# 192 rows of w_down as 96-row halves inside Strassen, with a fourth PSUM bank per pair, in an adaLN block of a spectral mixer and a SwiGLU feed-forward

## Chip, cores and metric

One core of one Trainium2 chip. The metric is the device time of one execution in microseconds (us), the median over runs.

## What is computed

```python
def _A_ref(x, w_r, w_i):                      # x: 1 x 2048 x 640
    X = rfft2(x.astype(float32))              # over (2048, 640), 321 columns kept
    X = X * (w_r + 1j * w_i)
    return irfft2(X, s=(S, D)).astype(bfloat16)

def _B_ref(x, w_gate, w_up, w_down):          # F = 1728
    return silu(x @ w_gate) * (x @ w_up) @ w_down

sa, ca, ga, sb, cb, gb = six 640-wide pieces of silu(c) @ w_mod
h = _layernorm(x) * (1 + ca) + sa
x = x + ga * _A_ref(h, A_w_r, A_w_i)
h = _layernorm(x) * (1 + cb) + sb
return x + gb * _B_ref(h, w_gate, w_up, w_down)
```

All inputs and the output are bfloat16. The 2048 tokens are 16 tiles of 128 (t = 0 to 15); 640 = 5 x 128; 1728 = 13 x 128 + 64 hidden columns.

## The kernel before

The order of instructions on every engine is written out by hand; each engine works through its own list in that order, and waits at an instruction until what it reads is there and what it overwrites is free.

**Spectral part (0 to 86 us).** The two FFTs are matrix products with tables. In the prologue (0 to 12 us) tables and x are loaded, the modulation columns are computed (`mod_cols`; `one_p_ca`, L433), and the first tiles' statistics are taken on DVE (`stats`, bn_stats L350, L351; `gram`, L368 to L372) and finished on POOL (a pow, L362). For each tile t the forward part (12 to 36 us) transforms along the 640 axis (L320, L323), subtracts the mean (`zout`, L390, DVE), scales a table by 1/std on POOL (`gscale`, L377, L378) and transforms along the tokens of a tile (`s1`, L398 to L401, four 324-column matmuls; copies L407). Behind the last tile SP transposes the result (L504); a DMA, L511, loads the rest of w_mod. The frequency part (36 to 63 us) runs over groups of frequencies: transposes (`t2_pe`, L523), `stage_a` (L551), the product with the filter on DVE (`prod`, L573), `stage_b` (L580), `stage_c` (L601); `ga_mod` (L634, L638) broadcasts the gate row ga over partitions between them. The filter's sums and mirrored rows are prepared by `wsum`, and by the DMAs of `flip` and `flip_edge`. The last loop (63 to 86 us) inverts tile by tile (`s1em` L645, `s1er` L650, copy L653 on ACT, L803 and L806 on PE), adds x on DVE (L808, result x1), and prepares the second layernorm (`ln2_sq` L726 on ACT, `ln2_var` L730 to L732, `ln2_pow` L736 on POOL, `ln2_xn`, a transposing DMA `ln2_tr`, and `ln2_mod` L762 on POOL or L765 on DVE). `wd_fold` (L791, DVE) multiplies rows of w_down by gb.

**Feed-forward part (86 to 255 us)**, in chunks of (first tile, tiles): (0,2), (2,4), (6,4), (10,4), (14,2). The first chunk is plain: 13 hidden blocks of 128 with a gate and an up product each (`gu_plain`, L1031, product L1037), then `down_plain` (L908, L912). The other chunks run two Strassen schemes. `gate_up_pairs` (L1058) makes hidden blocks 0 to 11 of gate and up in groups, by `step(i, g)`: matmuls into banks X, Y, Z, copies on ACT (L1084, L1090, L1097), sums and products on DVE (L1094, L1098, L1101, L1103, L1108). Its right-hand operands are sums of the normalised tokens, `h_sums` and `h_neg` (L996 to L1000, DVE), made in the chunk before. Hidden block 12 is done by `gu_plain` at the end of the chunk, and the last 64 hidden columns by `gu13`: 5 matmuls (L1010) that hold gate and up in one 128-row result; two Silus (L1015, L1017) on ACT and two copies (L1016, L1018) on DVE bring the halves of tokens side by side, ten small DMAs (L1019, L1020) cross partitions, and L1021 multiplies.

`down_pair` (L933) computes two token tiles at once: 12 hidden blocks are split in two halves of six (HK), the 640 outputs in two of 320. Seven products of 6 matmuls each, with sums S1 to S4 of the hidden activations (`a_sum`, L884 to L890, DVE) and T1 to T4 of w_down (`wd_tables`, L864 to L870). The remaining 192 rows (block 12, and the 64 rows of block 13) are 8 further matmuls, with one more sum S12 (L892) and a table W13 (`wd_rest`, L873 to L876): 50 matmuls per pair. Three PSUM banks X, Y, Z (of eight in a ring) hold a pair. ACT copies partial results out (L948, L955, L958, L964), POOL adds three of them to the rows of x1 (L949, L959, L962), and DVE adds the rest when storing (`out_store`, L898; DMA L899). Between the products `nxt(i)` puts the work for what follows on the engines: in the first pair of a chunk `a_sum` for the second pair, in the second pair `ln2_mod` and `h_sums` for the next chunk.

Of the kernel before, what the change touches and what calls it, by code (L numbers as in the profile page):

```python
# [28 lines left out]
IDLE = (3, 6, 1, 2)  # L29

# [125 lines left out]
def adaln_block_kernel(ctx, tc, A_x, A_w_r, A_w_i, B_x, B_w_gate, B_w_up, B_w_down, c, w_mod, out):  # L156
# [116 lines left out]
    nc.sync.dma_start(x_sb[:, 12:16, :], x_v[:, 12:16, :])  # L273
    flip_edge(A_w_i, Wflip[0])
    flip_edge(A_w_r, Wflip[1])
    flip(A_w_r, Wflip[1])
# [53 lines left out]
    if True:  # L330
# [62 lines left out]
        def s1(t, Z, Gs):  # L393
# [4 lines left out]
            nc.tensor.matmul(ar, lhsT=Gs[:, 0, :], rhs=zr, start=True, stop=False)  # L398
            nc.tensor.matmul(ar, lhsT=Gs[:, j, :], rhs=zi, start=False, stop=True)
            nc.tensor.matmul(ai, lhsT=Gs[:, 3 - j, :], rhs=zr, start=True, stop=False)  # L400
            nc.tensor.matmul(ai, lhsT=Gs[:, 0, :], rhs=zi, start=False, stop=True)  # L401
# [27 lines left out]
        t1(0)  # L429
        mps = psum[:, 7, 0:NC5]  # L430
# [12 lines left out]
        stats(0)  # L443
# [8 lines left out]
        gscale(0)  # L452
        stats(3)
        zout(0)
# [4 lines left out]
        for t in range(2, NT + 2):  # L459
# [27 lines left out]
            if t in (13, 15):  # L487
                for lo, hi in ((48, 64),) if t == 13 else ((0, 48), (64, 81)):
                    wsum(Wn, lo, hi, nc.vector)
# [7 lines left out]
    if True:  # L497
# [20 lines left out]
        def t2_pe(slot):  # L518
            ls = groups[slot] + (groups[4] if slot == 3 else [])
            n = len(ls)  # L520
            tp = banks((0, 1, 6, 7)[slot], 1, [8, 128], BF16)
# [3 lines left out]
            if slot == 0:  # L525
                nc.vector.tensor_tensor(B2[:], tp[:, :n, :], SAx[:], ALU.add)
            else:
                nc.scalar.copy(B2[:], tp[:, :n, :])
                nc.gpsimd.tensor_tensor(B2[:, 0:4, 0:1], B2[:, 0:4, 0:1], SA[:, ls[0]:ls[0] + 4].unsqueeze(2), ALU.add)
# [101 lines left out]
        def mod_bc(j, lo, bank, o=0):  # L631
            gps_ = psum[:, bank, o:o + 320]
            for k in range(NC5):
                nc.tensor.matmul(gps_, lhsT=sc_rep[:, k, :], rhs=wm_r[:, k, j, lo:lo + 320], start=(k == 0), stop=(k == NC5 - 1))  # L634
            return gps_

        def ga_mod(lo, bank):
            nc.scalar.copy(ga_bc[:, :, lo // 4:lo // 4 + 80], mod_bc(0, lo, bank).rearrange("p (m r) -> p r m", r=4))  # L638
# [18 lines left out]
        t2_pe(0)  # L657
        t2_pe(1)
# [4 lines left out]
        wsum(Wv, 48, 64, nc.vector)  # L663
# [3 lines left out]
        for g in range(NG + 1):  # L667
# [3 lines left out]
            if g + 2 < NG:  # L671
                PPs[g + 2] = stage_a(g + 2)[0]
            if g == NG - 3:
# [8 lines left out]
            if g in (1, 2):  # L682
                ga_mod(320 * (g - 1), 5 + g)
# [17 lines left out]
    nc.sync.dma_start(Wd_sb[:, 0:13, :], B_w_down[0:1664, :].rearrange("(fc fp) d -> fp fc d", fp=P))  # L701
    for h in range(2):
        nc.sync.dma_start(Wd_sb[64 * h:64 * h + 64, 13, :], B_w_down[1664:1728, :])
# [86 lines left out]
    def wd_fold(f2):  # L790
        nc.vector.tensor_tensor(Wd_sb[:, f2, :], Wd_sb[:, f2, :], gb_bc[:], ALU.mult)  # L791

    if True:
        VTs = {0: s1er(0), 1: s1er(1)}
        nc.vector.tensor_copy(gb_bc[:, 0:320], mod_bc(3, 0, 7))
        for t in range(NT):
            if t and t + 1 < NT:
                s1em(t + 1)
                VTs[t + 1] = s1er(t + 1)
            VT = VTs.pop(t)  # L800
            ops = banks(6 * (t % 2), 2, [4, 256])[:, :, 0:160]
            for h in range(2):
                nc.tensor.matmul(ops[:, 2 * h:2 * h + 2], lhsT=VT[:, 4, :], rhs=RI[:, 1, 2 * h:2 * h + 2, :],  # L803
                                 start=True, stop=False)
                for rr in range(2):
                    nc.tensor.matmul(ops[:, 2 * h + rr], lhsT=VT[:, 2 * h + rr, :], rhs=RI[:, 0, 2 * h + rr, :],  # L806
                                     start=False, stop=(rr == 1))
            nc.vector.scalar_tensor_tensor(x1[:, t, :].rearrange("p (m r) -> p m r", r=4), ops.rearrange("p r m -> p m r"), 1.0,  # L808
                                           x_sb[:, t, :].rearrange("p (m r) -> p m r", r=4), ALU.mult, ALU.add,
                                           accum_out=st2[:, t, 0:1])  # L810
            if t in (8, 11):
                gu_dma(GS[0][:], B_w_gate, t // 11 * 2, 2, t == 8)
            if 1 <= t <= 2:
                ln2_sq(t - 1)
            if t == 3:
                ln2_var(0, 2)
                ln2_pow(0, 2)
            if 4 <= t <= 5:
                ln2_xn(0, t - 4)
            if t == 5:  # L820
                ln2_tr(0)
                load_gu(1024, 1664)
            if t in (7, 9, 11, 13):
                ln2_sq(2 + (t - 7) // 2)
            if t == 10:
                ln2_mod(0)
            if t == 14:
                ln2_var(2, 4)
                ln2_pow(2, 4)
            if t >= 7 and t % 2:  # L830
                wd_fold((13, 0, 1, 2, 3)[(t - 7) // 2])
        for o, n, r, w in ((GS[2], 2, 0, B_w_gate), (UG.unsqueeze(1), 1, 4, B_w_gate), (GS[2], 2, 0, B_w_up), (UG.unsqueeze(1), 1, 4, B_w_up)):
            gu_dma(o[:], w, r, n, w is B_w_gate)

# [13 lines left out]
    S12 = rY.cut(6144, [128], F16)  # L848
    nh = rY.cut(6400, [4, 128])
    W13 = rH.cut(0, [2, 320])  # L850
# [419 lines left out]
```

## Time and profile before

| | us |
|---|---|
| median of 15 runs | 256.52 (255.87 to 257.7) |
| profiled execution | 256.71 |
| its span | 254.9 |

| stage, us of the span | bounds |
|---|---|
| prologue | 0 to 12 |
| forward tiles | 12 to 36 |
| frequency groups | 36 to 63 |
| inverse, x1 | 63 to 86 |
| chunk (0,2): gate/up, down | 86.2 to 100.3, to 107.7 |
| chunk (2,4): gate/up, pairs | 107.7 to 134.9, to 148.5 |
| chunk (6,4) | 148.5 to 175.8, to 189.4 |
| chunk (10,4) | 189.4 to 216.3, to 230.0 |
| chunk (14,2) | 230.0 to 243.8, to 251.7 |
| last sums and stores | 251.7 to 254.9 |

The granted clock of TensorE is 0.998. The engines are PE (TensorE; PEld is its weight loading), DVE (VectorE), ACT (ScalarE), POOL (GpSimd) and SP, which here only issues DMAs. In a timeline each row has the start, the length, the engine, the line, and what is written and read; in square brackets stands the idle time before it and what ended that.

### The profile page before, as it was taken

What the parts mean: (1) busy time and instruction counts of PE and PEld (TensorE: products, weight loads), DVE (VectorE), ACT (ScalarE), POOL (GpSimd) and SP (SyncE); (2) the same over time, 40 slices, a digit from 0 to 9 for tenths busy, and PEclk for the clock granted to TensorE, in tenths of its full rate; (3) what the DMA queues carried; (4) which work ended last, traced back from release to release, by engine and by line L of the source; (5) the groups of instructions that cost most, each with busy time, mean ns of one, the idle gap of its engine ahead of it and who ended that gap; (6) DMA issues with size and microseconds to landing.
All of it is one profiled execution on the core that took longest, in us unless ns stands there. A gap on an engine that the chain in (4) does not pass through costs nothing.

```text
span 254.9 us, 6501 instructions
## 1 busy us (share of the span) xinstructions
PE 244.5 (96%) x2520; PEld 199.4 (78%) x2520; DVE 208.3 (82%) x521; ACT 163.7 (64%) x305; POOL 73.0 (29%) x117
## 2 busy tenths in 40 slices
PE   8899988989999999999999999999999999999984
PEld 3688857979889887778876678886668886769953
DVE  2898888978889998879997996879995788994793
ACT  3788665978778598578963477773357776235730
POOL 4487745845021805000003600001440000440021
PEclk9999999999999999999999999999999999999999
DMA  7989999999999899610005020002411000212001
GB/s 222 390 271 336 298 394 194 246 259 399 319 344 290 223 257 173 133 36 0 3 0 105 29 75 13 3 3 46 96 41 36 3 0 4 51 51 59 4 0 51
DMA packets 46588, 34.78 MB, mean 136 GB/s; under 512 B 22111, under 2 KB 43486, under 8 KB 46174
## 3 DMA queue, kind: packets, MB, share of 16 engines
q1 hardware_dynamic: 44892, 30.36, 42.8%
q0 software_dynamic: 1376, 3.93, 6.8%
q8 instruction: 19, 0.31, 0.5%
q10 hardware_dynamic: 290, 0.08, 0.1%
q14 instruction: 11, 0.09, 0.1%
HBM read 26.80 MB, written 4.72 MB: 124 GB/s over the span
## 4 chain that ended last, share of the span: by engine, by line
PE 69%; DVE 5%; ACT 4%; DMA 3%; SPq 2%; issue 1%; DVEq 0%; ACTq 0%
PE psum L1058 29%; PE psum L933 17%; PE psum L1031 8%; DMA rM<-in_w_mod_dram 3%; PE psum L645 3%; SPq L504 2%; PE psum L803 2%; PE psum L580 2%; PE psum L806 2%; PE psum L912 1%; PE psum L551 1%; DVE rA L898 1%; PE psum L601 1%; PE psum L1010 1%; PE psum L650 1%
## 5 line engine op out<-in xcount | busy, mean ns | idle before, releaser
L1058 PEld LDWEIGHTS <-rW 128*128 128x128 bf16 (+1 forms) x528 | 47.0, 98 | 6.0 <-issue 0.6
L949 POOL TENSOR_TENSOR rM<-rM,rL 128x320 f32<-128x320 f32 x7 | 6.2, 885 | 86.8 <-ACT rL L948 86.8
L1058 PE MATMUL psum<-rE,rW 128*128 128x256 f16 (+1 forms) x192 | 27.7, 259 | 0.2 <-ACT rH L1090 0.2
L1058 PE MATMUL psum<-rW 128*128 128x256 bf16 (+1 forms) x240 | 27.1, 259 | 0.0
L573 DVE TENSOR_TENSOR rM<-psum,rW 128x384 bf16<-128x384 f32 (+2 forms) x42 | 20.4, 542 | 4.6 <-PE psum L551 3.8
L1058 PE MATMUL psum<-rY,rW 128*128 128x256 bf16 (+1 forms) x96 | 24.0, 259 | 0.0
L933 PEld LDWEIGHTS <-rX 128*128 128x128 bf16 (+1 forms) x181 | 16.1, 97 | 9.2 <-issue 1.6
L1031 PE MATMUL psum<-rW 128*128 128x256 bf16 (+1 forms) x170 | 23.2, 291 | 0.0
L933 PEld LDWEIGHTS <-rE 128*128 128x128 f16 x168 | 16.4, 98 | 6.5 <-DVE rE L884 0.2
L933 PE MATMUL psum<-rE 128*128 128x320 f16 x126 | 20.4, 299 | 0.0
L933 PE MATMUL psum<-rA,rX 128*128 128x320 bf16 (+1 forms) x119 | 19.5, 301 | 0.8 <-DVE rX L1037 0.8
L1031 PEld LDWEIGHTS <-rW 128*128 128x128 bf16 x170 | 16.5, 98 | 3.8
L1058 PEld LDWEIGHTS <-rE 128*128 128x128 f16 x192 | 17.4, 98 | 2.3
L1108 DVE TENSOR_TENSOR rX<-rH,rL 128x512 bf16<-128x512 bf16 x21 | 8.9, 425 | 11.7 <-ACT rL L1106 11.5
L736 POOL TENSOR_TENSOR rstd<-rstd,mhalf 128x4 f32<-128x4 f32 (+2 forms) x4 | 4.5, 1120 | 46.5 <-DVE rstd L732 46.5
L1098 DVE TENSOR_TENSOR rX<-psum,rX 128x512 f32<-128x512 f32 x21 | 14.5, 688 | 3.2 <-ACT rX L1097 2.9
L1097 ACT COPY rX<-psum 128x512 f32<-128x512 f32 x21 | 12.3, 587 | 7.2 <-PE psum L1058 7.1
L1094 DVE TENSOR_TENSOR rH<-psum,rW 128x512 bf16<-128x512 f32 x21 | 14.5, 690 | 2.4 <-PE psum L1058 0.6
L1090 ACT COPY rH<-psum 128x512 f32<-128x512 f32 x21 | 12.2, 581 | 6.4 <-PE psum L1058 5.7
L1084 ACT COPY rW<-psum 128x512 f32<-128x512 f32 x21 | 12.3, 586 | 5.8 <-PE psum L1058 5.8
L390 DVE SCALAR_TENSOR_TENSOR rE<-rE,mv,psum 128x648 bf16<-128x648 f32 (+1 forms) x17 | 14.1, 840 | 2.0 <-PE psum L323 1.6
L583 ACT CAST rY<-psum 128x512 bf16<-128x512 f32 (+2 forms) x21 | 11.8, 574 | 5.2 <-PE psum L580 5.1
(203 smaller groups left out, 667.6 us busy)
## 6 DMA issues: line engine op xcount, KB each, us to landing
out_dram<-rA SPq DMA_DIRECT2D x31, 80.0 KB, 1.6
rM<-in_w_mod_dram SPq DMA_DIRECT2D x3, 800.0 KB, 9.0
rA<-in_B_w_down_dram SPq DMA_DIRECT2D x1, 2080.0 KB, 13.7
rX<-in_A_x_dram SPq DMA_DIRECT2D x3, 640.0 KB, 7.2
rM<-in_w_mod_dram SPq DMA_DIRECT2D x1, 1600.0 KB, 8.2
rY<-in_B_w_gate_dram POOLq DMA_DIRECT2D x2, 768.0 KB, 6.7
rW<-in_B_w_gate_dram SPq DMA_DIRECT2D x2, 640.0 KB, 7.0
rW<-in_B_w_up_dram SPq DMA_DIRECT2D x2, 640.0 KB, 7.6
```

Source lines behind the costliest of these rows:

```text
L390: nc.vector.scalar_tensor_tensor(Zv[:, h], Cv[:, h], mv[:, t, 0:1], zps[:, h], ALU.mult, ALU.subtract)
L573: nc.vector.tensor_tensor(PP[:, :, hl], xv[:, :, hl], in1, ALU.mult)
L583: nc.scalar.copy(Y2[:, 0:n, :], yps[:, 0:n, :])
L933: nc.tensor.matmul(o, lhsT=lhsT, rhs=rhs, start=start, stop=stop, skip_group_check=True)
L1031: nc.tensor.matmul(gu[u], lhsT=Wgu[:, u, c5, ff * 128:(ff + 1) * 128], rhs=h2T[:, :, c5, :], start=(c5 == 0), stop=(c5 == NC5 - 1))
L1058: nc.tensor.matmul(o[:, f], lhsT=w, rhs=b, start=(start and f == 0 and i == 0), stop=(stop and f == F - 1 and i == len(ops) - 1), skip_gro ...
L1084: nc.scalar.copy(c0, X)
L1090: nc.scalar.copy(c2, X)
L1094: nc.vector.tensor_tensor(c11, Z, c0, ALU.add)
L1097: nc.scalar.copy(c3, X)
L1098: nc.vector.tensor_tensor(c22, Y, c3, ALU.add)
L1108: nc.vector.tensor_tensor(ato, v4(c11), v4(g21), ALU.mult)
```

## The change

- **w_down's last 192 rows** are two halves of 96 rows (`RK`): rows 1536 to 1631 in block 12, and rows 1664 to 1727 with rows 1632 to 1663 behind them in block 13. They become a seventh pair of blocks in the Strassen product: seven products of 7 matmuls, 49 per pair, with tables T7 (made by `wd_rest`) and sums S7 (`a_sum7`) of 96 rows. S12 and W13 go. A fourth bank W holds the last product of a pair, and POOL adds a fourth partial result to x1, except in the last pair, where DVE does it and W's first two blocks are done early.
- **gate/up.** `gu13` leaves gate and up where the matmuls put them: one Silu, and one DVE product of PSUM rows 64 to 127 with it. `gu_plain`'s block 12 is multiplied in two parts, 96 rows and 32 rows (`half.rest`). In chunk 0 `gu13` is issued ahead of the last x1 tile.
- **down_plain** has 14 matmuls of 128 or 96 rows per result, with no separate 64-row ones.
- **Prologue, last forward tile, first frequency groups, flip edges**: `stats(0)`, `zout(0)`, `wsum`, `ga_mod` and the flips move; `s1` of the last tile is computed in two column halves; `ln2_sq` goes two tiles earlier.

```diff
+    flip(A_w_r, Wflip[1])
     flip_edge(A_w_i, Wflip[0])
     flip_edge(A_w_r, Wflip[1])
-    flip(A_w_r, Wflip[1])
...
-            nc.tensor.matmul(ar, lhsT=Gs[:, 0, :], rhs=zr, start=True, stop=False)
-            nc.tensor.matmul(ar, lhsT=Gs[:, j, :], rhs=zi, start=False, stop=True)
-            nc.tensor.matmul(ai, lhsT=Gs[:, 3 - j, :], rhs=zr, start=True, stop=False)
-            nc.tensor.matmul(ai, lhsT=Gs[:, 0, :], rhs=zi, start=False, stop=True)
+            for h in (slice(0, 4),) if t < NT - 1 else (slice(0, 2), slice(2, 4)):
+                o = slice(81 * h.start, 81 * h.stop)
+                for a, ja, jb in ((ar, 0, j), (ai, 3 - j, 0)):
+                    nc.tensor.matmul(a[:, o], lhsT=Gs[:, ja, :], rhs=zr[:, h], start=(h.start == 0), stop=False)
+                    nc.tensor.matmul(a[:, o], lhsT=Gs[:, jb, :], rhs=zi[:, h], start=False, stop=(h.stop == 4))
...
         t1(0)
+        stats(0)
         mps = psum[:, 7, 0:NC5]
         mod_cols(mps, wm_ca, range(0, 3))
...
         t1(1)
-        stats(0)
         dfwd(0)
...
         gscale(0)
+        zout(0)
         stats(3)
-        zout(0)
...
+                    wsum(Wn, 64, 81, nc.gpsimd)
...
-            tp = banks((0, 1, 6, 7)[slot], 1, [8, 128], BF16)
+            tp = banks(slot % 2, 1, [8, 128], BF16)
...
+        wsum(Wv, 48, 64, nc.vector)
         t2_pe(1)
         PX = [stage_a(0)]
         t2_pe(2)
         PX.append(stage_a(1))
         t2_pe(3)
-        wsum(Wv, 48, 64, nc.vector)
+        ga_mod(0, 6)
+        ga_mod(320, 7, range(3))
         for g in range(2):
...
+            if g == 0:
+                ga_mod(320, 7, range(3, NC5))
...
-    nc.sync.dma_start(Wd_sb[:, 0:13, :], B_w_down[0:1664, :].rearrange("(fc fp) d -> fp fc d", fp=P))
-    for h in range(2):
-        nc.sync.dma_start(Wd_sb[64 * h:64 * h + 64, 13, :], B_w_down[1664:1728, :])
+    nc.sync.dma_start(Wd_sb[:, 0:12, :], B_w_down[0:1536, :].rearrange("(fc fp) d -> fp fc d", fp=P))
+    nc.sync.dma_start(Wd_sb[0:RK, 12, :], B_w_down[1536:1632, :])
+    nc.sync.dma_start(Wd_sb[0:64, 13, :], B_w_down[1664:1728, :])
+    nc.sync.dma_start(Wd_sb[64:RK, 13, :], B_w_down[1632:1664, :])
...
+    T7 = [rE.cut(37888 + 640 * i, [320], F16, parts=RK) for i in range(4)]
+    S7 = [rH.cut(256 * i, [128], F16, parts=RK) for i in range(4)]
...
-        nc.vector.memset(W13[0:64, 0], 0.0)
-        nc.vector.tensor_copy(W13[64:128, 0], Wd_sb[64:128, 13, 0:320])
-        nc.vector.tensor_copy(W13[0:64, 1], Wd_sb[0:64, 13, 320:640])
-        nc.vector.tensor_scalar_mul(W13[64:128, 1], Wd_sb[64:128, 13, 320:640], -1.0)
-
-    def a_sum(ATc, j, i, ks=slice(0, 6)):
-        a11, a12, a21, a22 = (ATc[:, HK * f + ks.start:HK * f + ks.stop, 256 * j + 128 * h:256 * j + 128 * h + 128]
-                              for h in range(2) for f in range(2))
-        s1, s2, s3, s4 = (x[:, ks] for x in (S1, S2, S3, S4))
+        b11, b12 = (Wd_sb[0:RK, 12, 320 * h:320 * h + 320] for h in range(2))
+        b21, b22 = (Wd_sb[0:RK, 13, 320 * h:320 * h + 320] for h in range(2))
+        tt = nc.vector.tensor_tensor
+        tt(T7[0], b12, b11, ALU.subtract)
+        tt(T7[1], b22, T7[0], ALU.subtract)
+        tt(T7[2], b22, b12, ALU.subtract)
+        tt(T7[3], b21, T7[1], ALU.subtract)
...
+    def a_sum7(ATc, j, i):
+        sums(i, S7, *(ATc[0:RK, 12 + f, 256 * j + 128 * h:256 * j + 128 * h + 128] for h in range(2) for f in range(2)))
...
-            if tl % 2 == 0:
-                pops = [[psum[:, next_banks(1), 0:320] for _ in range(2)] for _ in range(2)]
-                for h in range(2):
-                    for s in range(2):
-                        rows = slice(64 * s, 64 * s + 64)
-                        nc.tensor.matmul(pops[s][h], lhsT=ATc[rows, 13, 64 * tl:64 * tl + 128],
-                                         rhs=Wd_sb[rows, 13, 320 * h:320 * h + 320], start=True, stop=False)
             for h in range(2):
-                for fc in range(NFC - 1):
-                    nc.tensor.matmul(pops[tl % 2][h], lhsT=ATc[:, fc, tl * 128:(tl + 1) * 128],
-                                     rhs=Wd_sb[:, fc, 320 * h:320 * h + 320], start=False, stop=(fc == NFC - 2))
-                out_store(t0 + tl, pops[tl % 2][h], h)
+                pop = psum[:, next_banks(1), 0:320]
+                for fc in range(NFC):
+                    rows = slice(0, P if fc < 12 else RK)
+                    nc.tensor.matmul(pop, lhsT=ATc[rows, fc, tl * 128:(tl + 1) * 128],
+                                     rhs=Wd_sb[rows, fc, 320 * h:320 * h + 320], start=(fc == 0), stop=(fc == NFC - 1))
+                out_store(t0 + tl, pop, h)
...
+        W = psum[:, next_banks(1), 0:320]
+        last = t + 2 == NT
+        prod(X, half(0, ta), wd(0, 0), True, True)
         nc.scalar.copy(cps_[0], X)
         nc.gpsimd.tensor_tensor(xa[:, 0:320], xa[:, 0:320], cps_[0], ALU.add)
-        for k in range(3):
-            mm(Z, A12[:, k], B21[:, k])
-        prod(Y, S1, T1)
+        prod(Z, half(1, ta), wd(1, 0), True, ks=range(0, HK))
+        if last:
+            prod(W, half(1, tb), t7(3), True, ks=range(0, 2))
+        prod(Y, s7(0), t7(0), True, True)
         nxt(0)
-        mm(Y, ATc[:, 12, tb:tb + 128], w12(1), stop=True)
         nc.scalar.copy(cps_[1], Y)
-        prod(X, S2, T2, stop=True)
+        prod(Z, half(1, ta), wd(1, 0), stop=True, ks=(HK,))
+        prod(X, s7(1), t7(1), stop=True)
         nxt(1)
         nc.scalar.copy(cps_[2], X)
         nc.gpsimd.tensor_tensor(xb[:, 320:640], xb[:, 320:640], cps_[1], ALU.add)
-        prod(Y, S4, B22)
+        out_store(t, Z, 0)
+        prod(Y, s7(3), wd(1, 1), stop=True)
         nxt(3)
         nc.gpsimd.tensor_tensor(xa[:, 320:640], xa[:, 320:640], cps_[2], ALU.add)
-        prod(X, S3, T3, stop=True)
-        nc.scalar.copy(cps_[3], X)
+        prod(X, s7(2), t7(2), stop=True)
         nxt(2)
-        mm(Y, S12, w12(1))
         nxt(4)
-        mm(Y, r13, W13[:, 1], stop=True)
         out_store(t, Y, 1)
-        for k in range(3, HK):
-            mm(Z, A12[:, k], B21[:, k])
-        mm(Z, ATc[:, 12, ta:ta + 128], w12(0), stop=True)
-        out_store(t + 1, cps_[3], 1)
-        mm(X, ATc[:, 12, tb:tb + 128], w12(0))
-        mm(X, r13, W13[:, 0])
-        if t + 2 < NT:
-            prod(X, A22, T4, stop=True)
-            out_store(t, Z, 0)
-            out_store(t + 1, X, 0)
+        if not last:
+            nc.scalar.copy(cps_[3], X)
+            nc.gpsimd.tensor_tensor(xb[:, 0:320], xb[:, 0:320], cps_[3], ALU.add)
+            out_store(t + 1, cps_[3], 1)
+            prod(W, half(1, tb), t7(3), True, True)
+            out_store(t + 1, W, 0)
         else:
-            out_store(t, Z, 0)
+            nc.vector.tensor_tensor(xb[:, 0:320], X, xb[:, 0:320], ALU.add)
+            out_store(t + 1, X, 1)
             for lo in (0, 160):
-                prod(X[:, lo:lo + 160], A22, T4[:, :, lo:lo + 160], stop=True)
+                prod(W[:, lo:lo + 160], half(1, tb), [w[:, lo:lo + 160] for w in t7(3)], stop=True, ks=range(2, HK + 1))
             for lo in (0, 160):
-                out_store(t + 1, X[:, lo:lo + 160], 0, lo, 160)
+                out_store(t + 1, W[:, lo:lo + 160], 0, lo, 160)
 
...
-        gv = g13.rearrange("p (j s q) -> p s j q", s=2, q=128)
-        f13 = rX.cut(14336, [n // 2, 128], F32)
-        m13 = rX.cut(14336 + 1024, [n // 2, 128])
-        b13 = rX.cut(14336 + 1536, [n // 2, 128])
-        nc.scalar.activation(m13[0:64], gv[0:64, 1], ACT.Silu)
-        nc.vector.tensor_copy(m13[64:128], gv[64:128, 0])
-        nc.scalar.activation(f13[0:64], gv[0:64, 0], ACT.Silu)
-        nc.vector.tensor_copy(f13[64:128], gv[64:128, 1])
-        nc.sync.dma_start(b13[0:64], m13[64:128])
-        nc.sync.dma_start(b13[64:128], m13[0:64])
-        return lambda: nc.vector.tensor_tensor(ATc[:, 13, 0:64 * n], f13[:].rearrange("p j q -> p (j q)"),
-                                               b13[:].rearrange("p j q -> p (j q)"), ALU.mult)
+        sg13 = rX.cut(14336, [512], F32, parts=64)[:, 0:128 * n]
+        nc.scalar.activation(sg13, g13[0:64], ACT.Silu)
+        return lambda: nc.vector.tensor_tensor(ATc[0:64, 13, :], g13[64:128], sg13, ALU.mult)
...
+                if ff < 12:
+                    nc.vector.tensor_tensor(ATc[:, ff, :], gu[1], sg[:, 0:N], ALU.mult)
+                else:
+                    nc.vector.tensor_tensor(ATc[0:RK, 12, :], gu[1][0:RK], sg[0:RK, 0:N], ALU.mult)
+
+        half.rest = lambda: nc.vector.tensor_tensor(ATc[64:RK, 13, :], gu[1][RK:P], sg[RK:P, 0:N], ALU.mult)
...
         half(0)
         step(6, nG - 1)
+        q1, q2, q3, q4 = (lambda q=q: a_sum7(ATc, 0, q) for q in range(4))
         if n == 2:
-            step(5, nG - 1)
+            step(5, nG - 1, True)
+            half(1)
+            step(8, nG - 1)
             step(7, nG - 1)
             s3, s4 = later
             r1, r2, r3, r4 = (lambda q=q: a_sum(ATc, 0, q, slice(2, 6)) for q in range(4))
-            later[:] = [r1, r2, s4, r4, s3, r3]
-            half(1, lambda: run(2))
+            later[:] = [r1, half.rest, q1, r2, q2, s4, r4, q4, s3, r3, q3]
         else:
             queue(nG - 1)
             half(1, lambda: run(len(later) - 2))
-            run(2)
-            step(5, nG - 1)
-            step(7, nG - 1)
+            later[:0] = [half.rest, q1, q2]
+            later.extend([q3, q4, lambda: step(8, nG - 1), lambda: step(7, nG - 1)])
+            step(5, nG - 1, True)
         run(len(later))
-        a_sum(ATc, 0, 4)
...
+            if t == NT - 1:
+                fin13 = gu13(0, at_of(0))
...
+            if t in (5,7,9,11):
+                ln2_sq(2 + (5,7,9,11).index(t))
...
-                    if n == 4:
+                    if n == 4 and i < 4:
                         a_sum(ATc, 1, i)
+                        a_sum7(ATc, 1, i)
```

## The prediction

> **What bounds the kernel now.** I read the busy shares first, then the chain of waits, then what PE waits for, and last the windows of the feed-forward part and its timelines, because the change sits mostly there.
>
> ```profile
> PE 244.5 (96%) x2520; PEld 199.4 (78%) x2520; DVE 208.3 (82%) x521; ACT 163.7 (64%) x305; POOL 73.0 (29%) x117
> ```
>
> TensorE works for 244.5 of 254.9 us, so only about 10 us are idle and every matmul taken away counts almost in full, if nothing new makes PE wait. The chain of waits (start, length, what) shows where PE doesn't set the pace:
>
> ```profile
> 45.61 8.16 DMA rM<-in_w_mod_dram
> 53.81 0.28 PE psum L555 x5
> ...
> 84.26 0.59 ACT rL L653
> 84.89 0.31 PE psum L803
> ...
> 110.31 0.44 DVE rX L1016
> 110.77 0.38 ACT rX L1017
> 111.15 0.48 ACT rH L1090
> ```
>
> So the frequency stage hangs on a weight load that ends at 53.81; the end of the x1 loop waits for an ACT copy; and the 64-row rest of gate/up costs a little DVE/ACT ping-pong. The windows of the second chunk's two down pairs and of the next two pairs (window, length, busy us of PE, PEld, DVE, ACT and POOL, then clock, DMA share and GB/s):
>
> ```profile
> 134.90:141.70 6.80, 6.80 (x51) 4.68 (x50) 5.08 (x13) 1.70 (x4) 3.91 (x4) 1.00 0.52 99
> 141.70:148.50 6.80, 6.80 (x51) 4.81 (x51) 6.70 (x16) 4.60 (x8) 2.82 (x4) 1.00 0.16 49
> ...
> 175.80:182.60 6.80, 6.80 (x51) 4.67 (x50) 6.49 (x14) 1.71 (x4) 3.15 (x3) 1.00 0.51 96
> 182.60:189.40 6.80, 6.80 (x51) 4.81 (x51) 6.73 (x15) 3.87 (x7) 2.91 (x3) 1.00 0.16 51
> ```
>
> PE is full, but DVE is nearly full too in the second pair of each chunk (6.70 and 6.73 of 6.80). What DVE hasn't done by then (the next chunk's normalised tokens L765 and their sums L996 to L1000) PE needs in the next chunk's second step. And POOL isn't free beside DVE. Timelines of the two engines at the first pair:
>
> ```profile
> 139.10 0.85 POOL L949 TENSOR_TENSOR rM<-rM,rL 128x320 f32<-128x320 f32 x1
> 139.92 0.85 POOL L959 TENSOR_TENSOR rM<-rM,rL 128x320 f32<-128x320 f32 x1
> 140.75 1.17 POOL L962 TENSOR_TENSOR rM<-rM,rL 128x320 f32<-128x320 f32 x1
> ...
> 139.15 0.83 DVE L743 SCALAR_TENSOR_TENSOR nb<-st,rstd 128x6 f32<-128x6 f32 x1 [1.44 <-POOL rstd L736]
> 139.90 1.30 DVE L884 TENSOR_TENSOR rE<-rX 128x768 f16<-128x768 bf16 x1
> 141.30 1.03 DVE L886 TENSOR_TENSOR rE<-rE,rX 128x768 f16<-128x768 f16 x1
> 142.43 0.56 DVE L890 TENSOR_TENSOR rE<-rX,rE 128x768 f16<-128x768 bf16 x1
> ...
> 147.70 0.41 DVE L996 TENSOR_TENSOR rE<-rW 128x512 f16<-128x512 bf16 x1
> ...
> 149.28 0.29 DVE L1000 TENSOR_SCALAR rE<-rE 128x512 f16<-128x512 f16 x1
> ```
>
> The same 768-element sum takes 0.56 alone and 1.03 to 1.30 while a POOL add is under way.
>
> **What the Trainium skill says.** "SBUF — State Buffer", section "Who interferes with whom": a GpSimd instruction that reads SBUF and a DVE instruction with two SBUF inputs take the shared port in turn, the first blocks the other; a DVE source in PSUM isn't in it. The trace agrees: 0.56 becomes 1.03 to 1.30, and the PSUM store L898 keeps its 0.48. "TensorE: Matmul & The Clock Gate", section on LDWEIGHTS: the load is set by columns, not contraction rows, so a 96-row matmul should cost what a 128-row one does; in this trace the 64-row L933 matmuls run at nearly the 320-column pace of 0.136.
>
> **Part by part**, against the profiled execution (256.71, span 254.9; 0.19 over the median of 256.52).
>
> Prologue. The statistics of tile 0 (two bn_stats and an aggregate, 7.48 to 8.60, so 1.1) go ahead of one_p_ca L433, before which DVE idles 0.57: L433 is some 0.5 later. The first z (L390, 0.84) goes ahead of statistics 3, so the pow for tiles 2 and 3 and the second gscale come later on POOL. The first s1 matmuls follow that at 12.04 and 13.72, from where PE runs without a break. Between 0 (it is absorbed before 13.72) and +0.8; I take +0.5.
>
> The last s1 (t=15) in column halves can start when half of z is there; four 324-column matmuls stood behind L390's second half. Half of their 0.56: −0.27. Its ACT copies, SP's transposes and the load ending at 53.81 all follow it, so it is carried through; 0 if that load is bound by something else.
>
> First frequency groups, flip order on SP, and the sums moved to POOL: PE waits for the load at 53.81 whatever stands before it. The ga_mod matmuls (0.7 each) move, none is added. Cost 0; the cover is that load.
>
> Rest of gate/up for chunk 0 (L1010, 5 matmuls, 0.55) goes ahead of the last x1 tile. PE waits there 0.38 for L653, and two ACT squares (L726, 0.6 each) have left that stretch. Its input, POOL's L762, ends at 84.64, just in time: −0.5 (0 to −0.55).
>
> Down_plain: 4 row-tiled 64-row matmuls in 0.38 plus 52 become 56, of 0.136 each: 4 × 0.136 − 0.38 = +0.16.
>
> Rest of gate/up in the Strassen chunks: L1016, L1017, L1018, L1021 and ten small DMAs become one Silu and one DVE product from PSUM; PE's small gaps at 111.6 and 152.5 (matmuls start 0.24 and 0.34 later than the pace gives) close: −0.4 (0 to −0.6).
>
> Pairs: 50 matmuls become 49. A pair took 13.64/2 = 6.82, so 0.136 goes from each of the six full pairs: −0.84 with rounding (−0.8).
>
> Tail: the last pair has 2 full and 10 half-width matmuls for W where 12 half ones stood, S12 (0.88 beside POOL) is gone and so is a wait of PE for L1037 in part (0.78 at 247.06); against it stand four small sums and an added DVE add on X. −0.3, from −0.8 to +0.2.
>
> Without new stalls this is 0.5 − 0.27 − 0.5 + 0.16 − 0.4 − 0.84 − 0.3 = −1.65.
>
> Now DVE. In the stretch of a chunk's pairs L1016/L1018/L1021 are gone (1.3, but early in the chunk where DVE has time). New at the end of gate/up: the gate/up product of block 12 falls apart into a 96-row and a 32-row one, with the fixed cost and PSUM width of L1037 again: +0.6. The last c12 sum and its product (steps 8 and 7) go behind these; with four tiles they serve only the second pair, so 0. New: four 96x128 sums for each pair in place of one (L892, 0.21, net 0.14): +0.42 a pair. New on POOL: a fourth 128x320 add per pair, 0.86, which can hold up one sum (0.47 to 0.56 of delay).
>
> Walk for chunk 1 (pairs begin at P0 = 134.88). The +0.6 and +0.42 come ahead of the variance L730 to L732, so the pow L736 (1.32 on POOL) ends at about 140.1, where it ended at 139.1. The adds L949, L959, L962 and the new one are queued behind it, the sums for pair 1 behind L743 on DVE, which waits for pow. From 140.1 on four adds of 0.86 (3.4) alternate with four sums of 0.47 and four small ones of about 0.15 (2.5) and two stores (0.8): all done at 146.8. The fourth product needs its sum at P0 + 10.5 = 145.4, the fifth at 146.8: PE waits about 1.2 in pair 1 already. Then the stores, L765 (149.3 where it was 145.51, 2.3 long beside POOL) and L996 to L1000 (1.75) end at 153.3. PE needs them at 150.69 − 0.3 = 150.4. So a loss of 2.9 by the end of it (the 1.2 is in it). Bounds: 0.8, if POOL lets two DVE operations through between its adds, and 3.2.
>
> Chunk 2 has no pow in its way: L765 would begin at P0 + 10.65 for 7.96 and the sums end at P0 + 15.95, needed at 15.53: +0.45 (0 to 1). Chunk 3 has 3.0 of slack at this place (L1000 ends 228.6, needed 231.6): 0 (to 0.3).
>
> Sum: −1.65 + 2.9 + 0.45 = +1.7; 256.71 + 1.7 = 258.4, on the median's footing 258.2.
>
> **The rivals.** A, on the other side: DVE keeps up. It is decided at 150.4, where PE reads L999's and L1000's sums: if DVE is through them by then, PE never waits and the saved matmuls stay saved. For it: the small sums may slip in while PSUM-source operations run, and DVE has 1.7 us of idle in the first pair's window (5.08 of 6.80). Against: that idle is the wait for pow, which gets later. Time: 256.52 − 1.65 = 254.9.
>
> B: half of the stall, because two DVE operations run between POOL's adds: −1.65 + 1.7 = about 0, 256.6. For it: in the trace of before the four sums took 139.90 to about 143.4, 3.5 for 1.9 of work, so three adds cost 1.6 or 0.55 each, not 0.86; four would cost 2.2, and the sums end at 145.6. Against: before, only two of the four sums (L884, L886) met adds at all, and the new small ones give every add a partner.
>
> C: everything at its bad end: prologue +0.8, tail +0.2, stalls 3.2 + 1 + 0.3: 0.8 − 0.27 − 0.5 + 0.16 − 0.4 − 0.84 + 0.2 + 4.5 = +2.65, about 259.3; a fourth PSUM bank per pair (the ring of eight holds only two pairs) can make PE wait for a store on top.
>
> **How the numbers follow.** Forecast 0.45, A 0.24, B 0.13, C 0.18. A is faster, B is split (0.03 faster, 0.08 same, 0.02 slower, since 0.2% or 0.5 us is what a measurement here can tell), the forecast and C are slower but for 0.03 of same: faster 0.27, same 0.11, slower 0.62. Predicted 258.2. The range runs from A's time to above C's: 254.8 to 259.8; the forecast's own is 257.2 to 259.2.
>
> **What would show it.** Right: PE waits for DVE (L884 to L890's new sums, or L996 to L1000) at 145 to 153, two to three us in all, and for nothing at 84.9; POOL's adds and DVE's sums alternate at 140 to 146; chunk 1's pair 0 lasts 6.7. The forecast falls if the second chunk's pairs keep to 13.4 us and the third chunk starts without a wait, or if PE's idle time sits in the prologue or in a bank that isn't free yet.

## The result, and the profile after

| | before | after |
|---|---|---|
| median, us | 256.66 (47 runs) | 260.0 (9 runs) |
| ratio | | 1.0123, interval 1.0104 to 1.0142 |
| profiled execution's span | 254.9 | 258.2 |

The change makes the kernel slower by 1.2%, 3.3 us. The forecast was slower by 1.7 us, in a range that ended at 259.8: the direction and the largest term were right, the sum was about half of what came.

Where the two executions part can be read from a few instructions that both have. The table gives their start, and what the difference grew by in each stretch, beside what the prediction's terms add up to for it.

| first instruction of | before | after | grown by | predicted |
|---|---|---|---|---|
| the matmuls that need the last w_mod load (L555, now L561) | 53.81 | 55.10 | +1.29 | +0.23 |
| gate/up of chunk 0 (L1031, now L994) | 86.00 | 86.72 | −0.57 | −0.5 |
| gu13 of chunk 1 (L1010, now L982) | 108.17 | 108.97 | +0.08 | +0.16 |
| pairs of chunk 1 (L933, now L903) | 134.88 | 135.35 | −0.33 | −0.2 |
| pairs of chunk 2 | 175.77 | 178.66 | +2.42 | +2.42 |
| pairs of chunk 3 | 216.32 | 219.22 | +0.01 | +0.17 |
| the last pair | 243.76 | 246.66 | 0.00 | −0.28 |
| end of the span | 254.9 | 258.2 | +0.4 | −0.3 |

Three stretches went otherwise than predicted: the first, the end, and, smaller, the pairs of chunks 2 and 3. At the first row the load is later, and so is PE. The last w_mod load was issued at 46.06 and took 8.7, so it landed at about 54.8 (before: 45.61 and 8.2, so 53.8). PE came to it only at 55.10 and waited for nothing there:

```profile
55.10 0.27 PE L561 MATMUL psum<-sc_col,rM 128*128 128x1 bf16 x5
```

So about 1.0 of the 1.29 lay in the load whatever PE did before it, and 0.3 in PE's own delay behind the ga_mod matmuls, whose wait of 2.0 is the first in the list below. The page's first part after:

```profile
PE 245.8 (95%) x2516; PEld 200.7 (78%) x2516; DVE 214.8 (83%) x538; ACT 162.8 (63%) x299; POOL 81.1 (31%) x124
```

DVE works 6.5 us more than before and POOL 8.1 more. PE is idle for 2.0 us more, and busy for 1.3 us more although the change takes matmuls away; for some 3 us its clock was halved (last section). What PE waits for, after (total, times, longest):

```profile
PE psum L640 <- DMA rM<-in_w_mod_dram: 2.0, 1, 2.0
PE psum L1026 <- DVE rE L972: 1.1, 1, 1.1
...
PE psum L903 <- DVE rE L857: 0.8, 1, 0.8
PE psum L557 <- DVE rM L532: 0.7, 1, 0.7
PE psum L903 <- ACT rL L935: 0.4, 2, 0.2
```

L857 and L972 are the sum for the fifth product of chunk 1's second pair and the negation of the next chunk's token sums: the two waits that the prediction named. L640 (the ga_mod matmuls, which waited for nothing before) and the wait for L935 (an ACT copy) are new. The timelines of POOL, DVE and PE after, at chunk 1's pairs:

```profile
139.85 1.33 POOL L747 TENSOR_TENSOR rstd<-rstd,mhalf 128x6 f32<-128x6 f32 x1 [38.39 <-ACT rL L935]
141.16 0.85 POOL L925 TENSOR_TENSOR rM<-rM,rL 128x320 f32<-128x320 f32 x1
141.98 1.24 POOL L936 TENSOR_TENSOR rM<-rM,rL 128x320 f32<-128x320 f32 x1
143.19 1.31 POOL L940 TENSOR_TENSOR rM<-rM,rL 128x320 f32<-128x320 f32 x1
144.46 1.18 POOL L947 TENSOR_TENSOR rM<-rM,rL 128x320 f32<-128x320 f32 x1
145.59 1.18 POOL L925 TENSOR_TENSOR rM<-rM,rL 128x320 f32<-128x320 f32 x1
...
141.96 0.55 DVE L853 TENSOR_TENSOR rE<-rX 128x768 f16<-128x768 bf16 x1
142.43 0.88 DVE L853 TENSOR_TENSOR rH<-rX 96x128 f16<-96x128 bf16 x1
143.23 0.54 DVE L855 TENSOR_TENSOR rE<-rE,rX 128x768 f16<-128x768 f16 x1
143.70 0.88 DVE L855 TENSOR_TENSOR rH<-rH,rX 96x128 f16<-96x128 f16 x1
...
146.77 1.22 DVE L857 TENSOR_TENSOR rE<-rX 128x768 f16<-128x768 bf16 x1
147.92 0.88 DVE L857 TENSOR_TENSOR rH<-rX 96x128 f16<-96x128 bf16 x1
...
148.05 0.99 PE L903 MATMUL psum<-rE 128*128 128x320 f16 x6 [0.82 <-DVE rE L857]
...
154.00 0.61 PE L1026 MATMUL psum<-rE 128*128 128x256 f16 x4 [1.08 <-DVE rE L972]
```

The pow (L747) ends at about 141.17 and all adds queue behind it back to back, into the second pair's own. Beside them the 96x128 sums take 0.88 each, four times the 0.21 that they take alone. The fifth product (the one with the third sum; products are counted as in the prediction, without Z's) needs the sum L857, which is done at 147.99, and its small part at 148.8, while PE stands.

### The profile page after: what moved, and what is told of

Read it like the earlier page. It is cut to its first block, busy times and chain, and to the rows that moved or that the text cites. A ratio compares the mean times of both kernels' runs of the same rounds, so it can differ in the third digit from the quotient of the medians.

```text
span 258.2 us, 6499 instructions
## 1 busy us (share of the span) xinstructions
PE 245.8 (95%) x2516; PEld 200.7 (78%) x2516; DVE 214.8 (83%) x538; ACT 162.8 (63%) x299; POOL 81.1 (31%) x124
## 5 line engine op out<-in xcount | busy, mean ns | idle before, releaser
L1026 PEld LDWEIGHTS <-rW 128*128 128x128 bf16 (+1 forms) x528 | 47.0, 98 | 6.0 <-issue 0.7
L1026 PE MATMUL psum<-rE,rW 128*128 128x256 f16 (+1 forms) x192 | 27.7, 259 | 0.0
L1026 PE MATMUL psum<-rW 128*128 128x256 bf16 (+1 forms) x240 | 27.2, 259 | 0.3 <-DVE rW L776 0.2
L1026 PE MATMUL psum<-rY,rW 128*128 128x256 bf16 (+1 forms) x96 | 23.9, 259 | 0.0
L903 PEld LDWEIGHTS <-rE 128*128 128x128 f16 x168 | 16.1, 97 | 9.2 <-DVE rE L857 1.1
L994 PE MATMUL psum<-rW 128*128 128x256 bf16 (+1 forms) x170 | 23.2, 291 | 0.0
L903 PE MATMUL psum<-rE 128*128 128x320 f16 x126 | 20.7, 299 | 1.6 <-DVE rE L857 0.8
L1026 PEld LDWEIGHTS <-rE 128*128 128x128 f16 x192 | 17.3, 98 | 3.6 <-DVE rE L972 1.4
L994 PEld LDWEIGHTS <-rW 128*128 128x128 bf16 x170 | 16.5, 98 | 3.8
L747 POOL TENSOR_TENSOR rstd<-rstd,mhalf 128x4 f32<-128x4 f32 (+2 forms) x4 | 4.5, 1121 | 47.0 <-ACT rL L935 38.4
L903 PEld LDWEIGHTS <-rX 128*128 128x128 bf16 (+1 forms) x152 | 14.4, 97 | 5.6 <-DVE rX L1003 0.5
L903 PE MATMUL psum<-rA,rX 128*128 128x320 bf16 (+1 forms) x98 | 15.7, 299 | 0.0
L1026 PE MATMUL psum<-rE,rY 128*128 128x256 f16 (+1 forms) x96 | 15.1, 259 | 0.0
```

Of the source, the lines that this page charges most:

```text
L903: nc.tensor.matmul(o, lhsT=lhsT, rhs=rhs, start=start, stop=stop, skip_group_check=True)
L994: nc.tensor.matmul(gu[u], lhsT=Wgu[:, u, c5, ff * 128:(ff + 1) * 128], rhs=h2T[:, :, c5, :], start=(c5 == 0), stop=(c5 == NC5 - 1))
L1026: nc.tensor.matmul(o[:, f], lhsT=w, rhs=b, start=(start and f == 0 and i == 0), stop=(stop and f == F - 1 and i == len(ops) - 1), skip_gro ...
```

## The experiments

Each kernel ran beside the kernel before on the same chip; ratios are against it.

**1. ga_mod back in its place.** In the changed kernel the ten matmuls of ga_mod were returned to behind the second and third stage_b.

```diff
-        ga_mod(0, 6)
-        ga_mod(320, 7, range(3))
...
+            if g in (1, 2):
+                ga_mod(320 * (g - 1), 5 + g)
```

> The changed kernel with the ga_mod matmuls put back to where they were (5 each behind the second and third stage_b). Theory: in PE's list they stand ahead of stage_a(2), so everything behind them waits for the w_mod piece that lands at 41.5; and after 2 us of idle PE runs at half clock for 4 us. Then the frequency stage gives back 1.2 to 1.6 us (first stage_c matmul at about 45.1 where it is 47.64 now) and the kernel about 1.3. Rival: stage_a(2) would be late anyway, since DVE's filter sum took 2.05 beside POOL's and the next one waited for a mirrored row block until 39.10; then at most 0.4 us comes back.

Measured: 260.38, ratio 1.015 (1.0109 to 1.019); the changed kernel had 1.0123. The 1.3 us that the theory gave did not come: PE no longer waits at 41.5, the first stage_c matmul starts at 44.73 (expected 45.1), but then PE stands 1.87 us at the last w_mod load:

```profile
54.34 0.28 PE L561 MATMUL psum<-sc_col,rM 128*128 128x1 bf16 x5 [1.87 <-DMA rM<-in_w_mod_dram]
```

So that load covers all but some tenths of the move, much as predicted. What was overlooked is that the load itself is later.

**2. pow early.** The variance, pow and nb of tiles 10 to 15 go into the third and fourth group of chunk 1's gate/up, where POOL has nothing to do.

```diff
+            if ci == 1 and p == 2:
+                ln2_var(10, 6)
+                ln2_pow(10, 6)
+            if ci == 1 and p == 3:
+                ln2_nb(10, 6)
...
-        if ci == 1:
-            ln2_var(10, 6)
-            ln2_pow(10, 6)
-            ln2_nb(10, 6)
```

> The changed kernel with the variance, pow and nb of tiles 10 to 15 computed in the middle of chunk 1's gate/up, not ahead of its pairs. Theory: pow ahead of POOL's adds is what pushes all adds and sums of the pairs late, 141.2 where they could start from 137; without it the waits in pair 1 (0.98) and in the next chunk's step 2 (1.9) go for the larger part: 2 to 2.8 us less. Rival: it is the number of adds and sums in itself (DVE and POOL alternate, 8 sums and 4 adds per pair); then the waits shrink by under 1 us.

Measured: 256.92, ratio 1.0013 (0.9996 to 1.003): by the ratios 2.8 us less than the changed kernel, nearly the whole loss. In the profiles, chunk 1 from the start of its pairs to that of chunk 2's lasts 40.58, where it lasted 43.31 in the changed kernel and 40.89 before. PE waits for neither L857 nor L972 any more. POOL's adds now stand apart, each started when ACT's copy is there:

```profile
141.66 0.86 POOL L947 TENSOR_TENSOR rM<-rM,rL 128x320 f32<-128x320 f32 x1 [0.70 <-ACT rL L946]
143.62 0.86 POOL L925 TENSOR_TENSOR rM<-rM,rL 128x320 f32<-128x320 f32 x1 [1.11 <-ACT rL L924]
145.39 0.88 POOL L936 TENSOR_TENSOR rM<-rM,rL 128x320 f32<-128x320 f32 x1 [0.91 <-ACT rL L931]
```

The number of adds and sums is the same, so it is their time that cost 2.8 us. The edit moves two things at once: POOL's adds no longer stand behind the pow, and DVE's sums no longer behind nb (L754), which waited 1.45 for that pow. How much each of the two counts was not separated.

**3. Both of these at once.**

> Both edits at once. They lie in different stages, so the gains add up: theory 3.3 to 4.2 us, 255.8 to 256.7; rivals of both: under 1.4 us, 258.6 or more.

Measured: 257.74, ratio 1.0068 (1.0048 to 1.0087). A miss: 0.8 us slower than pow early alone, so beside the early pow ga_mod's new place is rather a gain. About half of this kernel's executions had a mean granted clock of 0.992 or 0.993, and of those all but one took 258.1 to 259.6, where most of the others took 257.1 to 257.7. The profiled one, at 256.66 the fastest of all, shows a clock of 0.50 from 40.6 to 44.0 and the first stage_c at 46.44 (44.73 in experiment 1), but the last load, passed at 54.16, hides most of that. Why the old place costs here stays open.

**4. The kernel before with ga_mod moved as in the change.**

> The kernel before with nothing but the ga_mod matmuls (and the banks of the transposes that they need) moved as in the change. Theory: the same loss as in the changed kernel, 1.2 to 1.6 us by the first stage_c and PE at half clock around 42 to 45. Of that a part is hidden, since PE waits 1.2 us at 53.81 for the next load anyway: so 0.2 to 0.6 us in the time. Rival: no loss, because the load is there in time when the mirrored rows go in the old order.

Measured: 257.04, ratio 1.0012 (0.9989 to 1.0034): no loss that can be told, though the interval doesn't exclude the theory's 0.2 to 0.6. The trace sides with the rival: PE waits 0.9 at the first piece and then 0.7 at the last load, where it waited 1.2 at that alone, its clock stays at 1.00, and the first stage_c starts at 44.95 for 44.97.

**5. Flips in the old order**, in the changed kernel.

```diff
-    flip(A_w_r, Wflip[1])
     flip_edge(A_w_i, Wflip[0])
     flip_edge(A_w_r, Wflip[1])
+    flip(A_w_r, Wflip[1])
```

> The changed kernel with the flip edges back ahead of the second flip on SP. Theory: that order is what makes every later transfer of SP's queue late by half a us to one us: the first w_mod piece is then issued at 30.7 where it is 31.2 now and lands at 40.7 (41.5), PE's wait for it shrinks from 2.0 to about 1.1 so that the clock isn't cut, and the last w_mod load lands at 53.7 (54.3): 0.6 us less, or up to 1.3 where the clock was cut. Rival: SP's order is without effect, since the loads are limited by the DMA engines' total work; then under 0.2 us.

Measured: 258.66, ratio 1.0073 (1.0038 to 1.0108), 1.3 us less than the changed kernel; the two intervals just touch. From SP's queue the first flip edge, the w_mod transfers and the transposes, changed kernel first, then this one:

```profile
13.19 5.01 SPq L262 DMA_DIRECT2D wflip_i<-in_A_w_i_dram  x1
...
20.26 0.58 SPq L278 DMA_DIRECT2D rM<-in_w_mod_dram  x1
...
31.20 0.57 SPq L286 DMA_DIRECT2D rM<-in_w_mod_dram  x1
37.12 8.89 SPq L509 DMA_TRANSPOSE rL<-rA  x3
46.06 1.00 SPq L516 DMA_DIRECT2D rM<-in_w_mod_dram  x1
```

```profile
12.60 0.95 SPq L262 DMA_DIRECT2D wflip_i<-in_A_w_i_dram  x1
...
17.21 1.80 SPq L278 DMA_DIRECT2D rM<-in_w_mod_dram  x1
...
30.72 0.62 SPq L286 DMA_DIRECT2D rM<-in_w_mod_dram  x1
37.22 7.98 SPq L509 DMA_TRANSPOSE rL<-rA  x3
45.24 0.85 SPq L516 DMA_DIRECT2D rM<-in_w_mod_dram  x1
```

The same three transfers stand ahead of L278 in both orders, but behind the second flip the issue of the first edge takes 5.0 us and not 0.95, and L278 goes out 3 us later. Most of this is made up again; the piece for ga (L286) is still issued 0.5 earlier in the old order, the transposes behind it finish 0.8 earlier, though they are issued later, so the last load (L516) goes out 0.8 earlier and PE gets to it at 53.38.

All 14 profiled kernels agree on the beginning: with the new order (7 kernels) the first edge took 4.5 to 5.0 and L278 was issued at 19.7 to 20.3; with the old order (7 kernels, before among them) 0.95 and 16.3 to 17.2. Further on the two groups come close: the piece for ga was issued at 30.7 to 31.2 and PE passed the last load at 53.6 to 55.1, mean 54.3, for 29.8 to 30.7 and 53.0 to 53.8, mean 53.3.

What an earlier load is worth depends on the next wait. In this profiled execution, the slowest of five (259.77), PE is 1.7 us ahead at the last load, but at gu13 of chunk 0 it waits for POOL's `ln2_mod`, 1.0 in three times, and at the first gate/up matmul only 0.24 is left:

```profile
84.75 0.27 PE L982 MATMUL psum<-rW,Wp 128*128 128x256 bf16 x1 [0.45 <-POOL rW L773]
```

**6. The new flip order alone, in the kernel before.**

> The kernel before with nothing changed but the second flip ahead of the flip edges. Theory: this order alone delays what follows in SP's queue: the piece for ga is issued 0.5 us later (31.2 for 30.7), the last w_mod load lands at 54.3 to 54.5 for 53.8, so 0.5 to 1 us slower. Rival: in the kernel before the order is hidden and only the other edits make it count; then within 0.2 us.

Measured: 257.07, ratio 1.0028 (1.0017 to 1.0039): 0.7 us slower by the ratio, the size that the theory gave. Its profiled execution doesn't show the theory's path: the first edge takes 4.54, but the piece for ga is issued at 30.68 (30.66 before) and the load passed at 53.88 (53.81). So the time bears out that the order costs something; on which path, this trace leaves open.

**7. A place of its own for the third copy.** In the changed kernel, cps_[2] goes to bytes 9216 on, which nothing uses any more there.

```diff
-    cps_ = [rL.cut((2560, 10496, 0, 1280)[i], [320], F32) for i in range(4)]
+    cps_ = [rL.cut((2560, 10496, 9216, 1280)[i], [320], F32) for i in range(4)]
```

> The changed kernel with the third copy of a pair (ACT, cps_[2]) in a place of its own. Theory: it shares bytes with the Silu results g21/g22 that step 7 reads; step 7 now stands behind the small sums on DVE, so ACT's copy waits for it, and PE waits for the copy ahead of the pair's fifth product, 0.36 us in each of chunks 2 and 3 (in chunk 1 a longer wait hides it): 0.7 us less, PE waits for the copy gone. Rival: the copy would wait for something else as late (POOL's adds, DVE's sum for that product), then 0 to 0.2 us.

Measured: 259.03, ratio 1.0096 (1.0065 to 1.0126), by the ratios 0.7 us less than the changed kernel, as the theory has it; the intervals overlap, so the trace has to decide. In the changed kernel, at chunk 2's first pair, DVE, ACT and PE read:

```profile
182.78 0.47 DVE L1075 TENSOR_TENSOR rX<-rH,rL 128x512 bf16<-128x512 bf16 x1
...
183.34 0.43 ACT L935 COPY rL<-psum 128x320 f32<-128x320 f32 x1 [1.31 <-DVE rX L1075]
...
183.81 0.97 PE L903 MATMUL psum<-rE 128*128 128x320 f16 x6 [0.20 <-ACT rL L935]
```

L1075 is step 7, which reads g22, and g22 begins in the bytes that the copy overwrites. PE's fifth product starts 0.50 after the last matmul of the fourth, where the pace is 0.14: 0.36 lost. With the copy elsewhere the wait is gone, and this pair lasts 6.70 (178.09 to 184.79) instead of 7.06 (178.66 to 185.72). Chunk 3 is shorter by the same 0.36.

**8. The fourth add on DVE.** In the changed kernel, for the full pairs.

```diff
-            nc.gpsimd.tensor_tensor(xb[:, 0:320], xb[:, 0:320], cps_[3], ALU.add)
+            nc.vector.tensor_tensor(xb[:, 0:320], X, xb[:, 0:320], ALU.add)
```

> The changed kernel with the fourth partial sum of the full pairs added by DVE from PSUM (0.4) and not by POOL. Theory: POOL's adds and DVE's sums take turns, so one add less in the first pair of chunk 1 brings the later sums forward by 0.8 to 1.2 and costs DVE 0.4: PE's waits in chunk 1 shrink by 0.3 to 0.8 us. Rival: what counts is DVE's own work; then 0.4 more for each pair whose sums are late, 0.4 to 0.8 us slower.

Measured: 259.18, ratio 1.0113 (1.0081 to 1.0145). PE's wait for L972 shrank from 1.1 to 0.5, that for a sum stayed at 0.8; from chunk 1's pairs to chunk 2's it is 42.67 for 43.31. The trace bears the theory out; the total is no different from the changed kernel's within the interval. One add less relieves a little, where the pow's place gives nearly all.

**9. pow early in the kernel before.**

> The kernel before with the pow of tiles 10 to 15 in the middle of chunk 1's gate/up. Theory: before had 1.1 us of slack at that place, PE never waited there, so nothing changes (within 0.2 us), though DVE's wait of 1.44 for pow goes; the place of pow costs only beside the new sums and adds. Rival: pow's place costs by itself (POOL's adds late, stores late): 0.5 us less or more.

Measured: 255.96, ratio 0.9992 (0.9968 to 1.0015): no change that can be told, though the interval alone doesn't exclude the rival's 0.5. The trace does: from chunk 1's pairs to chunk 2's it is 40.63 for 40.89. The pow was in the same place before and cost no more than these 0.26, because its delay ended inside the slack.

**10. Three repairs at once**: pow early, flips in the old order, own place for the copy.

> Three repairs at once: pow early, flips back, own place for the third copy. Theory: they lie in different places and add up, and with pow early the copy's wait counts in all three chunks (3 x 0.36): 256.9 - 0.6 - 1.0 = 255.3, faster than before by 0.4%. Rivals: if only the pow matters, 256.9; if the flips alone help, 256.3.

Measured: 254.98, ratio 0.9932 (0.9906 to 0.9958). Faster than before by 0.7%, 5 us better than the change as it was. In the list of PE's waits one alone is left from chunk 1 on, 0.4 in the last pair. Here the saved matmuls show: from pairs to pairs chunks 1, 2 and 3 last 40.19, 40.20 and 27.08, for 40.89, 40.55 and 27.44 before.

**11. The last pair in another order**, on top of 10: the fifth product and its DVE add ahead of the fourth. With it, the third sums come ahead of the fourth ones on DVE, and Z and W each have four blocks done early; this part of the edit is left out here.

```diff
+            prod(X, s7(2), t7(2), stop=True)
+            nc.vector.tensor_tensor(xb[:, 0:320], X, xb[:, 0:320], ALU.add)
+            out_store(t + 1, X, 1)
+            prod(Y, s7(3), wd(1, 1), stop=True)
+            out_store(t, Y, 1)
```

> The same with the last pair in another order: the fifth product ahead of the fourth, so that DVE's add of it falls into DVE's idle 1.05 us and not ahead of the last stores. Theory: the tail is bound by DVE (add 0.4, stores 0.4 and 2 x 0.27 behind the last products), so 0.4 to 0.6 us less than the kernel beside it, 254.8. Rival: the end is set by the first sums of that pair (PE waits 0.7 for them) and by the last transfer, then 0 to 0.2.

Measured: 255.05, ratio 0.9938 (0.9922 to 0.9953): no gain over 10, as the rival had it. From the pair's first matmul to the end of DVE's last store 8.45 us passed for 8.65: the add and all four stores still stand one behind another at the end (247.82 to 249.78).

**12. Without the last add**, on top of 10.

```diff
-            nc.vector.tensor_tensor(xb[:, 0:320], X, xb[:, 0:320], ALU.add)
```

> The kernel with the three repairs, with the last pair's DVE add of the third product's sum into x1 left out (that part of the last tile's output lacks it). Theory: DVE is the bound behind the last products, so its 0.40 comes off whole. Rival: the last matmuls or the transfers on SP set the end, 0 to 0.15 us.

Measured: 254.6, ratio 0.9927 (0.9905 to 0.9948); the interval can't tell 0.4 us from nothing, but the trace can. With the add, then without it:

```profile
247.86 0.49 DVE L873 TENSOR_TENSOR rA<-psum,rM 128x320 bf16<-128x320 f32 x1 [1.05 <-POOL rM L940]
248.27 0.48 DVE L952 TENSOR_TENSOR rM<-psum,rM 128x320 f32<-128x320 f32 x1
248.67 0.94 DVE L873 TENSOR_TENSOR rA<-psum,rM 128x320 bf16<-128x320 f32 x3
```

```profile
249.08 1.35 DVE L873 TENSOR_TENSOR rA<-psum,rM 128x320 bf16<-128x320 f32 x4 [1.05 <-POOL rM L940]
```

DVE waits for POOL's last add (L940), and from there its work follows without a gap, so DVE is the bound. It ends 8.65 us after the pair's start with the add (240.96 to 249.61) and 8.25 without (242.18 to 250.43): 0.40, and the span from the pair's start to the end is 0.3 shorter.

## Why the prediction was wrong

**Right: the stall in chunk 1, with its place and its total.** Predicted was +2.9 by a chain through pow, POOL's adds and DVE's sums. The stretch grew by 2.42 where the terms gave 2.42, and PE's matmuls start later than the pace of the first pair (6.70) gives: by 1.6 up to the end of the pairs, and by 1.2 more at L1026. The steps between are off: the sums of pair 1 end at 148.8 and not 146.8, since the pow ended later and three of the second pair's adds joined in, and `ln2_mod` (L776) took 1.69 for 2.3 and made a part of it up. So the exact total is partly luck. Experiment 2 takes nearly the whole of the stall away by moving variance, pow and nb, and experiment 9 shows that their place costs next to nothing without the new sums and adds. The 96-row matmuls keep the pace of 0.14, as the prediction took it.

Rival B (half of the stall) is out by size, but its picture holds in part: at the first two adds a small and a large sum do run for each, a round of 1.27 where the two take about 0.6 alone. An estimate from this is 0.67 for an add, between the forecast's 0.86 and B's 0.55. Rival A, no stall, came only with experiments 2 and 10.

**Wrong: "Cost 0; the cover is that load."** This was said of the first groups, the flips and ga_mod together. The step looked at PE's list and not at the queue that the cover itself stands in: the load landed 1.0 later. At the matmuls that need it the difference was +1.29 where +0.23 was predicted. For ga_mod the cover held, but for the last 0.3 in this execution (experiments 1 and 4). For the flips it did not: experiments 5 and 6 put 1.3 and 0.7 us on their order. What is shown of the way there is the flip edge of 4.5 to 5.0 us in SP's queue; how it comes to 1 us at the last load is not. Part of the 1.29 belongs to the two profiled executions: before's was the latest of its group, after's the latest of its own.

**Wrong: steps 8 and 7 behind the sums, "so 0".** I asked who reads their result, and not whose bytes they read. A copy that needs those bytes became late and PE with it, 0.36 in the first pairs of chunks 2 and 3 (experiment 7). It ate up the saved matmuls there. **Wrong the other way: chunk 2, +0.45.** That stall didn't come: in experiment 7, without the late copy, the stretch to the pairs of chunk 3 lasts 40.19 for 40.55 before. The two errors nearly cancel: +0.01 and 0.00 grew where +0.17 and −0.28 were expected.

**Mis-sized: the tail, −0.3, measured +0.4.** Behind the last products DVE has one add more (0.40, experiment 12), and the last stores wait for DVE, not for PE. That is 0.4 of the 0.7; the rest is open. The prediction's bad end was +0.2.

**Mis-sized, the other way: the prologue, +0.5.** In the traces the first s1 starts at 11.86 for 12.04 before, and the second at 13.54 for 13.72: no loss here. (Of the ten profiled kernels with the change eight start it by 12.12, two at 12.58 and 13.61; this was not followed up.) The split of the last s1 gave less than its 0.27: its transposes start 0.31 earlier, but 0.18 of this was there at the first s1. The term for gu13 of chunk 0 (−0.57 for −0.5) holds as long as POOL's `ln2_mod` is in time, which it is not in experiment 5.

**The range.** Its upper end was set by rival C, whose sum is wrong by 1: the terms 0.8 − 0.27 − 0.5 + 0.16 − 0.4 − 0.84 + 0.2 + 4.5 give +3.65 and not +2.65, so 260.4, or 260.2 on the median's footing, and not 259.3. With this a range that ends above C would have held 260.0, but by luck: C lays the loss on larger stalls, a slow prologue and a fourth bank, and gives the two costs of nothing no bad end at all.

## What to carry to other kernels

When a step is hidden behind a transfer, ask also what the change does to that transfer: everything ahead of it in its queue counts, and the order of it too. When an instruction is moved back, list the buffers that it reads and who writes into them next, not only who waits for its result. And a slow operation that heads an in-order queue (pow, 1.3 us) is harmless while there is slack behind it; it makes all that follows arrive in a bunch, and where two engines then take turns each operation waits for its partner (here a sum of 0.21 took 0.88), so move it to where its engine is idle before adding work behind it. Last, add up the bad end a second time.

## What was unexpected of the hardware

After PE stood idle for 2.0 us from 39.6 on, its granted clock fell to half for 3.2 us (41.8 to 45.0). Windows of the changed kernel (window, length, busy us of PE, PEld, DVE, ACT and POOL; the clock is the third number from the end):

```profile
39.60:41.50 1.90, 0.00 (x0) 0.00 (x0) 1.78 (x4) 0.80 (x1) 1.23 (x4) 1.00 1.36 105
41.50:42.50 1.00, 0.95 (x5) 0.61 (x5) 0.00 (x0) 0.00 (x0) 0.55 (x1) 0.64 1.28 291
42.50:43.50 1.00, 1.00 (x6) 0.54 (x5) 0.00 (x0) 0.43 (x1) 0.00 (x0) 0.50 1.21 150
43.50:44.50 1.00, 1.00 (x7) 0.85 (x6) 0.17 (x1) 0.00 (x0) 0.70 (x2) 0.50 1.26 277
```

It doesn't happen each time, and the length of the wait doesn't decide it. The kernels of experiments 2, 7 and 8 waited 1.94, 1.85 and 1.71 us at the same place in their profiled executions and kept their clock. That of experiment 3 fell to 0.50 for 3.4 us after a wait of only 1.17. Among the 20 executions of experiment 2 the 7 with a mean clock of 0.990 or 0.993 had a median of 257.47 and the others 256.84; in the changed kernel the 4 with 0.991 to 0.993 had 260.1 and the others 259.8. What brings the cut stays open.
